# Linear attention and SwiGLU, four layers in one core: keys of two tiles from centred rows, 1/std inside phi, and phi of the last queries ahead of the first products with 1/den

## The chip, the cores and the metric

One core of a Trainium2 chip runs the whole program in one launch. The metric is device microseconds (us) of that launch; single launches of one kernel agree within about 0.3% here, and all runs below are of the fast state (granted clock 0.999 to 1.0). "PE" is TensorE, "PEld" its weight loads, "DVE" VectorE, "ACT" ScalarE, "POOL" GpSimd, "SP" SyncE, which issues most transfers. The span of a profile is some 2 us shorter than the launch time.

## The reference

Four layers on 2048 rows of 512 numbers, in bf16: linear attention (32 heads of 16), SwiGLU, and both again with the same weights.

```python
def _A_ref(x, wqkv, wo):                       # layers 0 and 2, on layernorm(x)
    q, k, v = split(x @ wqkv)                  # 32 heads of 16
    phi = lambda t: jnp.where(t > 0, t + 1, jnp.exp(t)) + 1e-6
    pq, pk = phi(q), phi(k)
    kv  = einsum("bhsd,bhse->bhde", pk, v)     # sum over all rows
    z   = einsum("bhsd->bhd", pk)              # sum over all rows
    num = einsum("bhqd,bhde->bhqe", pq, kv)
    den = einsum("bhqd,bhd->bhq", pq, z)[..., None] + 1e-6
    return (num / den) @ wo
def _B_ref(x, w_gate, w_up, w_down):           # layers 1 and 3, on layernorm(x)
    return (silu(x @ w_gate) * (x @ w_up)) @ w_down
x = x + _A_ref(_layernorm(x)); x = x + _B_ref(_layernorm(x)); ...   # twice
```

## The kernel before

The rows stand as 16 tiles of 128. The kernel is a list of operations in a fixed order: `PROGRAM` orders TensorE, and one list for each other engine orders that engine. An engine does its list strictly in order, so one instruction that waits holds up all behind it. Tokens read *layer, kind, tile*: `0k4` is the key product of tile 4 in layer 0, `t` a transpose on TensorE, `g` the sum G of (phi of keys) x rows, `q` queries, `d` den, `m` KV x Wo, `w` the output product, `u` gate and up, `n` down, `S` a dummy product that keeps the array busy. On the other engines, `0q23.phi` is the last step of phi for block 23 of the queries, `0d0.pqn2` a product of phi(q) with 1/den, `0G1.evac` a copy of G out of PSUM, `i.ld` a weight load, `i.c7` the last step of a constant mask.

```python
# layer norm of one tile (cut): statistics, then rows scaled by 1/std, then a transpose
op("dve", lambda v: v.bn_stats(...)); op("dve", lambda v: v.bn_aggr(...))        # mean, variance
op(vp_on, lambda p: p.tensor_scalar(out=vpe[:, t:t + 1], ..., scalar2=1e-5, ...)) # + eps
op("pool", lambda p: p.tensor_tensor(out=rstd[:, t:t + 1], ..., op=ALU.pow))      # ** -0.5
op("dve", lambda v: v.tensor_scalar(out=b_ap, in0=X[:, t, :], scalar1=mean,
                                    scalar2=rstd[:, t:t + 1], op0=sub, op1=ALU.mult))
# tiles 0 to 3 of layer 0 are transposed on TensorE and copied out; all others by a DMA transpose on SP

def phi(pb, dst, dk, name):
    op("act", lambda a: a.activation(out=etmp[e][:], in_=PB[pb][:], func=ACT.Exp), ...)
    if on_act:
        op("act", lambda a: a.activation(out=dst, in_=PB[pb][:], func=ACT.Identity, bias=onep[:]), ...)
    op("dve", ...)      # min(exp, 1) + 1e-6
    op("dve", ...)      # max with t + 1

# den (cut): 1/den is replicated over a head's 16 columns on ACT, transposed by DMA, multiplied on DVE
op("act", ... out=rrep ..., kind="rep"); op("sp", ... dma_start(RT..., rrep, transpose=True))
op("dve", ... out=pq, in0=pq, in1=RT, op=ALU.mult, kind="pqn")

# z (cut): Zm is z times the head mask; every den product needs it
op("dve", lambda v: v.tensor_tensor(out=Zm[:], in0=PB[pb]..., in1=mask[:]..., op=ALU.mult), kind="zm")
```

Of the kernel before, what the change touches and what calls it, by code (L numbers as in the profile page):

```python
# [164 lines left out]

PROGRAM = """
S S S S S S S S S S S S S S S S S S S S S S S S S S S S S S S S S S S S S S S S S S 0t0 S S S S S S S S 0k0 S S S S
0t1 S S S 0t2 S S S 0k1 0k2 S 0t3 0g0 0g1 0k3 0g2 0k4 0k5 0g3 0k10 0g4 0k9 0g5 0k6 0k7 0q03 0z0 0g10 0z4 0k8 0k15
0g7 0k13 0k12 0g9 0k11 0z2 0z10 0z9 0q11 0z3 0z5 0z8 0z15 0g6 0z13 0k14 0q02 0z7 0q10 0q01 0q00 0z1 0g11 0q12 0q21
0z14 0z12 0z6 0z11 0q13 0d02 0d03 0d01 0d00 0g8 0q20 0d11 0q22 0g13 0d12 0d13 0d10 0q23 0d20 0g15 0g12 0g14 0d23  # L170
0d22 0d21 0q30 0v 0q31 0m0 0m1 0m2 0m3 0r2 0w3 0w2 0q33 0w1 0w0 0w5 0w11 0q32 0w7 0w6 0w9 0d33 0w8 0w4 0w10 1u011
1u007 1u005 1u008 1u002 1u006 0d31 0d32 1u012 1u003 1u013 0d30 1u010 1u004 1u000 1u110 1u001 1u009 1n3 0w14 1n0 0w12
1u106 1n1 1u102 1n2 1u107 1u204 0w13 1u101 0w15 1u111 2k2 1u109 1u105 1u103 1u104 1u108 2k0 1u100 2k1 2q00 1u112
1u113 2k3 1n7 1u209 1n6 1u211 1u205 1n4 1n5 1u213 1u200 1u303 1u202 1u203 2q10 1u301 1u208 1u309 1u304 1u206 1u212
2g0 1u201 1u311 1u302 2q11 1u305 1u207 1u310 2q01 1u308 2q03 1u312 2q02 1u210 1n11 1u313 2k4 1u300 1n8 1n10 1u306
1n9 1u307 2k8 1n14 2k7 2k10 2k5 2q21 1n15 2k6 2k9 2k11 1n13 1n12 2q12 2k15 2k14 2g3 2g5 2q20 2q22 2k13 2q23 2g2 2k12
2g7 2g6 2g14 2q13 2s 2d01 2g12 2d02 2g1 2d00 2d03 2d20 2d13 2d21 2q30 2d22 2d10 2d12 2d11 2g13 2q31 2g10 2d23 2g15
2g4 2g9 2g11 2g8 2r1 2q32 2v 2q33 2m0 2m1 2m2 2m3 2d31 2d30 2w0 2w1 2w2 2d32 2w3 2w6 2w5 2w11 2d33 2w4 2w8 2w7 2w9
2w10 3u008 3u000 3u009 3u013 3u010 3u004 3u003 3u005 3u007 3u103 3u110 3u108 3u012 3u002 3u001 3u006 3u104 2w13
3u011 3n3 3u100 2w12 3n2 3n0 3u106 3u105 2w14 3u107 3u111 3n1 3u102 3u109 3u112 3u101 3u113 3n6 3n4 3n5 3n7 3u200  # L180
3u201 3u202 3u203 3u204 2w15 3u205 3u206 3u207 3u208 3u209 3u210 3u211 3u212 3u213 3n8 3n9 3n10 3n11 3u300 3u301
3u302 3u303 3u304 3u305 3u306 3u308 3u307 3u309 3u310 3u311 3u312 3u313 3n12 3n13 3n14 3n15
# [4 lines left out]
i.ld i.ld1 0x2.stats 0x2.sq 0x7.stats 0k0.exp 0t1.xT 0t2.xT 0x10.stats 0k1.exp 0x10.sq 0k2.exp 0t3.xT 0x15.stats  # L187
0x12.stats 0x7.sq 0k3.exp 0x15.sq 0x12.sq 0k4.exp 0k5.exp 0x13.stats 0x13.sq 0k10.exp 0k10.id1 0k9.exp 0k9.id1
0x14.stats 0x14.sq 0k6.exp 0k7.exp 0k6.id1 0q03.exp 0x11.apply 0k8.id1 0k8.exp 0k15.exp 0k15.id1 0k13.exp 0k12.exp
0k13.id1 i.c 0k11.exp 0q11.id1 i.c1 0q11.exp 0k14.id1 0k14.exp 0q02.exp 0q02.id1 0q10.exp 0q01.id1 0q01.exp 0q00.exp  # L190
i.c3 0q12.id1 0q12.exp i.c2 0q21.exp 0q21.id1 0q13.id1 0q13.exp 0d0.rep 0d0.rep2 0q20.exp 0d0.rep1 0q22.exp 0d0.rep3
0q23.exp 0q23.id1 0d1.rep1 0G0.evac 0G2.evac 0G3.evac 0d1.rep 0q30.id1 0q30.exp 0q31.exp 0q31.id1 0M1.evac 0M3.evac
0d1.rep3 0d1.rep2 1x3.sq 1x2.sq 0q33.id1 1x1.sq 0q33.exp 1x0.sq 0q32.exp 1x5.sq 0q32.id1 1x11.sq 1x7.sq 1u011.tanh
1u007.tanh 1x6.sq 1u005.tanh 1u008.tanh 1u002.tanh 1u006.tanh 1x6.apply 1x9.sq 1u012.tanh 1u003.tanh 1u013.tanh
1x4.sq 1u010.tanh 1u004.tanh 1u000.tanh 1x10.sq 0d3.rep2 1u110.tanh 1u001.tanh 0d3.rep 1u009.tanh 1x8.sq 1x10.apply
1x8.apply 1x14.sq 2x3.sq 0d3.rep1 0d3.rep3 2x1.sq 1u102.tanh 1u106.tanh 1u107.tanh 2x2.sq 1u204.tanh 1u101.tanh
2x0.sq 1x13.sq 2k2.id1 1u111.tanh 2k2.exp 1u109.tanh 1u105.tanh 1u103.tanh 2x1.apply 1u104.tanh 1u108.tanh 1x12.sq
2k0.exp 2k0.id1 2k1.id1 2q00.id1 2k1.exp 1u100.tanh 1u112.tanh 1u113.tanh 2q00.exp 1x15.sq 2k3.id1 2k3.exp 2x7.sq
1u209.tanh 2x6.sq 1u211.tanh 1x13.apply 2x4.sq 1u205.tanh 2x6.apply 1u213.tanh 2x5.sq 2x7.apply 1u200.tanh
1u303.tanh 2x5.apply 1u203.tanh 1u202.tanh 2q10.id1 2q10.exp 1u301.tanh 1u208.tanh 1u309.tanh 1u304.tanh 1u206.tanh  # L200
1u212.tanh 1u201.tanh 1u311.tanh 1u302.tanh 2q11.id1 2q11.exp 1u305.tanh 1u207.tanh 1u310.tanh 2q01.exp 2q01.id1
1u308.tanh 2q03.exp 2q03.id1 1u312.tanh 2q02.exp 2q02.id1 1u210.tanh 1u313.tanh 2k4.exp 1u300.tanh 2x11.sq 2k4.id1
2x8.sq 1u306.tanh 2x10.sq 2x8.apply 1u307.tanh 2x9.sq 2x10.apply 2x9.apply 2k8.id1 2k8.exp 2k7.exp 2x14.sq 2k7.id1
2k10.exp 2q21.id1 2k5.id1 2k5.exp 2q21.exp 2k6.exp 2x14.apply 2k9.exp 2x15.sq 2k11.exp 2k9.id1 2x13.sq 2q12.exp
2k15.exp 2x12.sq 2k15.id1 2k14.exp 2q20.exp 2k13.exp 2q22.exp 2q23.id1 2q22.id1 2k12.exp 2q23.exp 2q13.id1 2q13.exp
2d0.rep 2d0.rep1 2d0.rep2 2q31.exp 2q30.exp 2d0.rep3 2q31.id1 2d2.rep 2G0.evac 2G2.evac 2G3.evac 2q32.id1 2d2.rep1
2q32.exp 2d2.rep2 2M0.evac 2M1.evac 2M2.evac 2q33.exp 2q33.id1 2d2.rep3 3x0.sq 3x2.sq 3x1.sq 3x3.sq 3x6.sq 3x5.sq
3x11.sq 3u008.tanh 3u000.tanh 3u009.tanh 3x7.sq 3u013.tanh 3u010.tanh 3x4.sq 3u004.tanh 3u003.tanh 3u005.tanh
2d3.rep 3u103.tanh 2d3.rep1 3u007.tanh 3x9.sq 3u110.tanh 3x8.sq 3u108.tanh 2d3.rep2 3u002.tanh 3u012.tanh 3u001.tanh
2d3.rep3 3u006.tanh 3u104.tanh 3u011.tanh 3u100.tanh 3x13.sq 3x12.sq 3u106.tanh 3u105.tanh 3u107.tanh 3u111.tanh  # L210
3x10.sq 3x13.apply 3u109.tanh 3x10.apply 3u102.tanh 3u101.tanh 3u113.tanh 3u112.tanh 3u200.tanh 3u201.tanh
3u202.tanh 3u203.tanh 3u205.tanh 3u204.tanh 3u207.tanh 3u206.tanh 3u208.tanh 3u209.tanh 3x15.sq 3x14.sq 3u211.tanh
3u210.tanh 3u212.tanh 3u213.tanh 3u300.tanh 3u301.tanh 3u302.tanh 3u303.tanh 3u304.tanh 3u306.tanh 3u305.tanh
3u307.tanh 3u308.tanh 3u309.tanh 3u310.tanh 3u312.tanh 3u311.tanh 3u313.tanh
""",
    "dve": """
i.c 0x0.stats 0x0.aggr 0x0.vpe 0x1.stats 0x1.aggr 0x0.apply 0x3.stats 0t0.xT 0x4.stats 0x3.aggr 0x4.aggr 0x1.apply
0x2.apply 0x5.stats 0k0.ts 0x4.apply 0x5.aggr 0k0.phi 0x3.apply 0x9.stats 0k1.ts 0k1.phi 0x9.aggr 0k2.ts 0x5.apply
0k2.phi 0x6.stats 0x10.apply 0x6.aggr 0x9.apply 0x8.stats 0k3.ts 0k3.phi 0x7.vpe 0x6.apply 0x8.aggr 0k4.ts 0k4.phi
0x7.apply 0k5.ts 0k5.phi 0x12.vpe 0x8.apply 0k10.ts 0k10.phi 0x11.stats 0x11.aggr 0x15.apply 0x11.vpe 0x13.apply  # L220
0x12.apply 0x14.vpe 0k7.ts 0k6.ts 0k7.phi 0q03.ts 0k9.ts 0k9.phi 0k6.phi 0q03.phi 0x14.apply 0k8.ts 0k12.ts 0k15.ts
0k8.phi 0k15.phi 0k12.phi 0k13.ts 0k11.ts 0k13.phi 0k11.phi 0k14.ts 0q11.ts 0q02.ts 0k14.phi 0q11.phi 0q02.phi
0q10.ts 0q10.phi 0q01.ts 0q01.phi 0q00.ts 0q00.phi 0z.zm 0q12.ts 0d0.den 0d0.den1 0q13.ts 0q12.phi 0q13.phi 0q21.ts
0q21.phi 0q20.ts 0q20.phi 0d1.den 0q22.ts 0d1.den1 0q22.phi 0q23.ts 0d0.pqn2 0q23.phi 0G1.evac 0d0.pqn1 0d2.den
0d2.den1 0d0.pqn3 0v.mask 0q30.ts 0d2.den2 0d1.pqn1 0M0.evac 0M2.evac 0d0.pqn 0r2.pqn 0w3.res 0r2.pqn1 0w2.res
0r2.pqn2 1x3.apply 0r2.pqn3 0w1.res 1x2.apply 0w0.res 0d1.pqn3 0d1.pqn2 0q33.ts 1x1.apply 0q33.phi 0d1.pqn 0w5.res
1x0.apply 0w11.res 0w9.res 1x5.vpe 0w7.res 0w6.res 0q32.ts 1x5.apply 0w4.res 1x11.vpe 0w10.res 1x7.vpe 1u011.gst
0w8.res 1u011.h 0q31.ts 1x11.apply 0q31.phi 0q30.phi 1u007.gst 1u007.h 1x6.vpe 1u005.gst 1u008.gst 1u008.h 1u005.h
0q32.phi 1u006.gst 1u006.h 1u002.gst 1u002.h 1u012.gst 1x7.apply 1u012.h 1u003.gst 1x4.vpe 0d3.den 1x4.apply 1u003.h
1x9.apply 1u013.gst 0d3.den1 1u013.h 1u010.gst 1u010.h 1u004.gst 1u004.h 1u000.gst 1u000.h 1u001.gst 1u001.h  # L230
1u009.gst 1u009.h 1u110.gst 0d3.pqn 0d3.pqn2 0w14.res 1u110.h 1n3.res 0d3.pqn3 1n1.res 1u102.gst 1n0.res 0w12.res
# [57 lines left out]
""",  # L289
}  # L290


PE_T = set("""
0d2 0t0 0t1 0t2 0t3 2d1 2z
""".split())
# [13 lines left out]
def bass_interleave_layers__linear_attn_block__swiglu_ffn__prompt_kernel(  # L309
# [20 lines left out]
    with stack:  # L330
# [144 lines left out]
        def ln(L, t):  # L475
# [3 lines left out]
            if (L, g) not in slot_of:  # L479
                slot_of[L, g] = r_xt.take(NF if L % 2 else 2 * TG)  # L480
# [75 lines left out]
        def xt_keys(L, g):  # L556
            return [f"xt{slot_of[L, g]}_{i}" for i in range(TG)]
# [84 lines left out]
        def z_acc(L, t):  # L642
            if L not in zb:
                zb[L] = [bank(pin=True), 0]
# [280 lines left out]
```

## Time and profile before

| | before |
|---|---|
| time, median of 3 | 429.98 us (429.4 to 430.33) |
| span of the profile | 428.1 us |
| first key product starts | 7.07 us |
| key product of tile 4 starts | 15.69 us |
| last mask step ends, first den product starts | 42.20, 42.56 us |
| first output product of layer 0 (`0w`) | 56.60 us |
| sum z of layer 2 starts, G x Wqkv of layer 2 starts | 248.05, 261.35 us |
| last product starts | 424.95 us |

These start times are milestones: the same product in every variant. Times without a unit are us from the start of the profile. A difference between two kernels is read from the stretch between two milestones in which it arises. The profile lines that carry the reading stand in the prediction. One more line of the page was not thought of then and matters later. It is in the table of DMA queues (queue, kind, packets, MB, share of 16 engines), and it counts 17 instruction fetches (blocks of the program that an engine reads in) of 16 KB. I take them for TensorE's own instruction stream; the counts behind that stand below.

```profile
q8 instruction: 17, 0.28, 0.3%
```

### The profile page before, as it was taken

The numbers are of one execution on the slowest core, as the hardware profiler recorded it, in microseconds if no ns is written. First come the engines' busy times: TensorE is split into PE (matmuls) and PEld (weight loads), VectorE is DVE, ScalarE is ACT, GpSimd is POOL, SyncE is SP. The second block draws the span as 40 slices with busy tenths as digits, with TensorE's granted clock in tenths as the row PEclk, the third lists the DMA queues (instruction fetches are blocks of the program that an engine reads in).
The fourth block names the chain that finished last, engine by engine and source line by source line (L and its number), as shares of the span: only waits on it lengthen the run. The fifth ranks groups of instructions, "written<-read, shape, count | busy, mean of one in ns | idle before, by whom it ended". The sixth has DMA issues, their size and how long they took to land.

```text
span 428.1 us, 6340 instructions
## 1 busy us (share of the span) xinstructions
PE 419.4 (98%) x2219; PEld 195.5 (46%) x2219; DVE 287.8 (67%) x629; ACT 202.9 (47%) x399; POOL 83.0 (19%) x205
## 2 busy tenths in 40 slices
PE   8999899999999999999999999999999999999997
PEld 6444444444444444444444444344444444444443
DVE  6865799793675476875447869888837606853662
ACT  5998785563356264254465648445312302402220
POOL 5634035210120150001334500431002000100000
PEclk9999999999999999999999999999999999999999
DMA  8639534522011021000021113322110010021001
GB/s 277 141 75 329 126 64 101 146 50 51 4 22 37 2 52 34 2 0 2 2 48 26 25 26 63 62 46 41 38 38 0 13 51 25 0 63 37 2 0 50
DMA packets 53279, 23.21 MB, mean 54 GB/s; under 512 B 46528, under 2 KB 52160, under 8 KB 53248
## 3 DMA queue, kind: packets, MB, share of 16 engines
q1 hardware_dynamic: 51408, 16.27, 17.6%
q0 software_dynamic: 1296, 6.03, 4.1%
q10 hardware_dynamic: 544, 0.52, 0.4%
q8 instruction: 17, 0.28, 0.3%
q14 instruction: 14, 0.11, 0.1%
HBM read 9.70 MB, written 2.10 MB: 28 GB/s over the span
## 4 chain that ended last, share of the span: by engine, by line
PE 88%; DMA 5%; ACT 3%; DVE 2%; issue 1%; SPq 0%; POOL 0%; ACTq 0%; DVEq 0%
PE pb L409 88%; DMA RT<-rrep 2%; DMA xnT<-xnA 1%; DMA X<-in_A_x_dram 1%; ACT pq L567 1%; ACT etmp L564 1%; ACT rrep L719 0%; DVE pq L573 0%; ACT GT L657 0%; DVE pq L732 0%; SPq L723 0%; ACT xnA L498 0%; SPq L440 0%; DVE xnA L522 0%; ACT xnA L495 0%
## 5 line engine op out<-in xcount | busy, mean ns | idle before, releaser
L782 ACT ACTIVATE tht<-pb 128x512 f32<-128x512 f32 x112 | 65.4, 595 | 129.4 <-PE pb L409 106.8
L409 PE MATMUL pb<-xnT,Wg 128*128 128x512 bf16 x448 | 115.0, 379 | 0.6 <-issue 0.6
L409 PE MATMUL pb<-xnT,Wu 128*128 128x512 bf16 x448 | 115.0, 379 | 0.0
L784 DVE SCALAR_TENSOR_TENSOR tht<-tht,pb 128x512 f32<-128x512 f32 x112 | 75.4, 684 | 55.6 <-ACT tht L782 48.9
L409 PE MATMUL pb<-Wd,hT 128*128 128x512 bf16 (+2 forms) x462 | 99.8, 373 | 0.0
L787 DVE TENSOR_TENSOR hT<-tht,pb 128x512 bf16<-128x512 f32 x112 | 74.2, 682 | 2.8
L409 PEld LDWEIGHTS pb<-Wd,hT 128*128 128x128 bf16 x462 | 44.7, 98 | 52.3 <-DVE hT L787 0.2
L409 PEld LDWEIGHTS pb<-xnT,Wu 128*128 128x128 bf16 x448 | 43.6, 98 | 53.1 <-DVE hT L787 0.8
L409 PEld LDWEIGHTS pb<-xnT,Wg 128*128 128x128 bf16 x448 | 43.5, 98 | 53.3 <-issue 1.3
L511 POOL TENSOR_TENSOR rstd<-vpe,negh 128x1 f32<-128x1 f32 x64 | 37.4, 587 | 90.4 <-DVE vpe L507 88.3
L564 ACT ACTIVATE etmp<-pb 128x512 bf16<-128x512 f32 x64 | 37.2, 594 | 21.8 <-PE pb L409 13.1
L501 POOL TENSOR_SCALAR mv<-sums 128x1 f32<-128x1 f32 x55 | 12.8, 239 | 119.8 <-DVE X L810 62.1
L409 PE MATMUL pb<-Wqkv,xnT 128*128 128x512 bf16 x128 | 31.2, 379 | 1.2 <-DMA xnT<-xnA 0.6
L409 PE MATMUL pb<-xnT,Wqkv 128*128 128x512 bf16 x128 | 32.1, 379 | 0.0
L409 PE MATMUL pb<-pk,xnA 128*128 128x512 bf16 x128 | 31.2, 379 | 0.0
L409 PE MATMUL pb<-GT,pq 128*128 128x512 bf16 x128 | 30.2, 379 | 0.2
L498 ACT ACTIVATE xnB<-X,sums 128x512 bf16<-128x512 bf16 x32 | 22.9, 717 | 15.7 <-DVE X L762 8.8
L569 DVE TENSOR_SCALAR etmp<-etmp 128x512 bf16<-128x512 bf16 x64 | 18.7, 304 | 12.1 <-ACT etmp L564 12.0
L762 DVE SCALAR_TENSOR_TENSOR X<-pb,X 128x512 bf16<-128x512 f32 x32 | 21.6, 686 | 7.1 <-PE pb L409 7.0
L810 DVE SCALAR_TENSOR_TENSOR X<-pb,X 128x512 bf16<-128x512 f32 x16 | 11.0, 689 | 19.1 <-PE pb L409 19.0
L498 ACT ACTIVATE xnA<-X,sums 128x512 bf16<-128x512 bf16 x23 | 16.5, 717 | 12.1 <-DVE X L810 11.9
L810 DVE SCALAR_TENSOR_TENSOR pq<-pb,X 128x512 bf16<-128x512 f32 (+2 forms) x17 | 10.9, 656 | 14.4 <-PE pb L409 14.3
(77 smaller groups left out, 309.9 us busy)
## 6 DMA issues: line engine op xcount, KB each, us to landing
out_dram<-pq SPq DMA_DIRECT2D x15, 128.0 KB, 1.8
Wg<-in_B_w_gate_dram POOLq DMA_DIRECT2D x4, 448.0 KB, 4.9
Wu<-in_B_w_up_dram POOLq DMA_DIRECT2D x4, 448.0 KB, 4.6
X<-in_A_x_dram SPq DMA_DIRECT2D x6, 256.0 KB, 4.8
Wd<-in_B_w_down_dram POOLq DMA_DIRECT2D x3, 512.0 KB, 4.7
Wqkv<-in_A_wqkv_dram SPq DMA_DIRECT2D x2, 512.0 KB, 7.0
Wqkv<-in_A_wqkv_dram ACTq DMA_DIRECT2D x2, 256.0 KB, 3.5
X<-in_A_x_dram SPq DMA_DIRECT2D x4, 128.0 KB, 3.4
```

The lines of the kernel that those rows point to most:

```text
L409: return op("pe", lambda e: e.matmul(o_ap, lhsT=lhsT, rhs=rhs, start=start, stop=stop, skip_group_check=skip), r=r, w=w, n=n)
L498: op("act", lambda a: a.activation(out=b_ap, in_=X[:, t, :], func=ACT.Square, scale=-float(D), bias=sums[:, t:t + 1], accum_out=mv[:, t, 1 ...
L501: op("pool", lambda p: p.tensor_scalar(out=mv[:, t, 0:1], in0=sums[:, t:t + 1], scalar1=-1.0 / D, scalar2=None, op0=ALU.mult), r=[f"sm{t}" ...
L511: op("pool", lambda p: p.tensor_tensor(out=rstd[:, t:t + 1], in0=vpe[:, t:t + 1], in1=negh[:], op=ALU.pow), r=[f"vp{t}", "negh"], w=[f"rs{ ...
L564: op("act", lambda a: a.activation(out=etmp[e][:], in_=PB[pb][:], func=ACT.Exp), r=[f"pb{pb}"], w=[f"e{e}"], kind="exp")
L567: op("act", lambda a: a.activation(out=dst, in_=PB[pb][:], func=ACT.Identity, bias=onep[:]), r=[f"pb{pb}", "onep"], w=dk, kind="id1")
L569: op("dve", lambda v: v.tensor_scalar(out=etmp[e][:], in0=etmp[e][:], scalar1=1.0, scalar2=1e-6, op0=ALU.min, op1=ALU.add), r=[f"e{e}"], w ...
L762: op("dve", lambda v: v.scalar_tensor_tensor(out=X[:, t, :], in0=PB[pb][:], scalar=1.0, in1=X[:, t, :], op0=ALU.mult, op1=ALU.add, accum_o ...
L782: op("act", lambda e: e.activation(out=tht[a][:], in_=PB[pg][:], func=ACT.Tanh, scale=0.5), r=[f"pb{pg}"], w=[f"th{a}"], kind="tanh")
L784: op("dve", lambda v: v.scalar_tensor_tensor(out=tht[a][:], in0=tht[a][:], scalar=1.0, in1=PB[pg][:], op0=ALU.add, op1=ALU.mult), r=[f"pb{ ...
L787: op("dve", lambda v: v.tensor_tensor(out=hT[h][:, j, :], in0=tht[a][:], in1=PB[pu][:], op=ALU.mult), r=[f"pb{pu}", f"th{a}"], w=[f"h{h}_{ ...
L810: op("dve", lambda v, pb=pb, lo=lo, hi=hi: v.scalar_tensor_tensor(out=o_ap[:, lo:hi], in0=PB[pb][:, 0:hi - lo], scalar=0.5, in1=X[:, t, lo ...
```

## The change

Its intent: start the first key products earlier by leaving 1/std out of the way to them; take away the stop of 1.33 us near 50 us; shorten the waits around z and the output product of layer 2.

```diff
+            if f"{L}c{t}" in PE_T:                      # tiles 0 and 1 of layer 0: rows minus mean only
+                op("dve", lambda v: v.tensor_scalar(out=pq[3][:, t, :], in0=X[:, t, :], scalar1=mean, scalar2=None, op0=sub), ...)
...
-        def phi(pb, dst, dk, name):
+        def phi(pb, dst, dk, name, by=1.0, rk=()):      # by = rstd of the tile
-            op("act", lambda a: a.activation(out=etmp[e][:], in_=PB[pb][:], func=ACT.Exp),
+            op("act", lambda a: a.activation(out=etmp[e][:], in_=PB[pb][:], func=ACT.Exp, scale=by),
-                op("act", lambda a: a.activation(out=dst, in_=PB[pb][:], func=ACT.Identity, bias=onep[:]),
+                op("act", lambda a: a.activation(out=dst, in_=PB[pb][:], func=ACT.Identity, bias=onep[:], scale=by),
...
 PROGRAM, head ("S*42" stands for 42 tokens S)
-S*42 0t0 S*8 0k0 S*4 0t1 S*3 0t2 S*3 0k1 0k2 S 0t3 0g0 0g1 0k3 0g2 0k4
+S*27 0c0 S*8 0k0 S*3 0c1 S*3 0t2 0k1 0t3 S*3 0k2 0k3 S 0g0 0g1 0g2 0k4
 PROGRAM, layer 2
-2s 2d01 2g12 2d02 ... 2m3 2d31 2d30 2w0 2w1 2w2
+2s 2g12 2d01 2d02 ... 2m3 2w0 2d31 2d30 2w2 2w1
 order of VectorE, layer 0
-0d1.den 0q22.ts 0d1.den1 0q22.phi 0q23.ts 0d0.pqn2 0q23.phi 0G1.evac 0d0.pqn1 0d2.den 0d2.den1 0d0.pqn3 0v.mask
+0d1.den 0d1.den1 0q23.ts 0q22.ts 0q22.phi 0d0.pqn 0q23.phi 0G3.evac 0d2.den 0d0.pqn2 0d2.den1 0d0.pqn1 0v.mask
 order of ScalarE, layer 0
-0q22.exp 0d0.rep3 0q23.exp 0q23.id1 0d1.rep1 0G0.evac 0G2.evac 0G3.evac 0d1.rep
+0q22.exp 0q23.exp 0q23.id1 0d0.rep3 0G0.evac 0G2.evac 0G1.evac 0d1.rep1 0q30.id1 0d1.rep
... (cut: the head of the other lists, layer 2's keys and queries, layer 3; two more DMA transposes, 0x0.xT and 0x1.xT)
```

## The prediction

> **What bounds the kernel now.** I read the page's busy table first, then its chain of waits, then the waits of PE alone, then the PE, DVE and ACT timelines where the chain leaves PE.
>
> ```profile
> PE 419.4 (98%) x2219; PEld 195.5 (46%) x2219; DVE 287.8 (67%) x629; ACT 202.9 (47%) x399; POOL 83.0 (19%) x205
> ...
> PE 88%; DMA 5%; ACT 3%; DVE 2%; issue 1%; SPq 0%; POOL 0%; ACTq 0%; DVEq 0%
> ```
>
> PE is the bound: 98% busy and 88% of the chain that ended last. The 98% contains dummy products at the start (42 in one piece, `pb<-hT`) that only keep the array running, so PE's free time is better counted from the timeline. In steady state four 128x512 products start every 0.864 us (123.73, 124.59, 125.45), 0.216 us each. Adding the column counts of all matmuls other than the dummies at 2.4 GHz gives 407 us. So of the 428.1 us span about 21 us is not needed by the products. Some 7 us of it lie before the first key product at 7.07, 3 us after the last matmul start (424.9), and the rest is dummies, per-matmul overhead (2.5 ns x 2000 = 5 us) and waits. The waits are what a change of order can win:
>
> ```profile
> PE pb L409 <- DVE pq L573: 1.3, 1, 1.3
> ...
> PE pb L409 <- DMA xnT<-xnA: 0.6, 1, 0.6
> PE pb L409 <- DVE xnT L553: 0.5, 1, 0.5
> PE pb L409 <- DVE GT L633: 0.4, 1, 0.4
> PE pb L409 <- DVE Zm L614: 0.4, 1, 0.4
> PE pb L409 <- DVE pq L750: 0.3, 1, 0.3
> ```
>
> The first, 1.3 us, is the largest wait of PE in the kernel and falls at 50.5. The chain of waits (start, length, piece) and below it the timeline (start, length, engine, line, operands, idle before) show where it comes from:
>
> ```profile
> 46.51 4.53 DMA RT<-rrep
> 51.04 0.02 issue
> 51.06 0.04 DVE pq L732
> 51.10 0.31 issue
> 51.40 0.43 DVE pq L573
> ```
>
> ```profile
> 51.06 0.43 DVE L732 TENSOR_TENSOR pq<-pq,RT 128x512 bf16<-128x512 bf16 x1 [1.83 <-DMA RT<-rrep]
> ...
> 51.40 0.42 DVE L573 TENSOR_TENSOR pq<-pq,etmp 128x512 bf16<-128x512 bf16 x1
> ...
> 51.88 0.46 PE L409 MATMUL pb<-Zm,pq 128*128 128x8 bf16 x12 [1.33 <-DVE pq L573]
> ```
>
> DVE works in program order. The last step of phi of query 23 (L573, 0.42 us) had its inputs by 49.4, but stands behind a product with 1/den (L732) that waits for the second transposed 1/den tile, landed at 51.04. DVE stood idle for 1.83 us and PE with it. ACT too: its copies of G (L657) began at 51.64, behind a replicate (L719) that waited for a buffer held by the same transpose. That transpose took longer than its neighbours (48.79 to 51.04 from its first to last engine, others 0.15 to 0.2 us); one 16 KB instruction fetch ran on a DMA engine just then. So part of this wait is luck.
>
> At the head, the chain runs over loads and the first DMA transpose:
>
> ```profile
> 9.80 5.84 DMA xnT<-xnA
> 15.65 0.05 issue
> 15.69 25.94 PE pb L409 x176
> ```
>
> From 15.69 PE runs dense to 42. What counts at the head is therefore when the key product of tile 4 starts, and how much was finished before it.
>
> **What the Trainium skill says.**
> - "TensorE: Matmul & The Clock Gate", Part 1: back to back products start every 107 ns for 128 columns while the clock is cold and every 55.6 (128) or 215.7 ns (512) warm, and the array warms after some 3.4 us of sustained work. The trace agrees: the dummies start 107 ns apart until 5.27 us, then 56 ns; 512 columns take 216 ns.
> - "ScalarE: Activation LUTs", What ACT_TABLE_LOAD costs: each per-partition pointer operand adds about 93 ns to an ACTIVATE. The trace agrees: exp with immediates is 0.60 us, Identity with a pointer bias 0.68. Exp with 1/std as scale should be near 0.68, Identity with both near 0.78.
> - "DMA: Bandwidth & Descriptors", Queues, rings and completion order: descriptors on an engine's ring are taken in ring order. The trace agrees as far as it shows: the first transpose is issued at 9.80, but the last weight load on the same queue lands at 13.74 and the transpose at 15.65.
>
> **The change, part by part.**
> 1. *Keys of tiles 0 and 1 from centred rows.* For the first tile it takes out, on the path to the keys, the +eps (0.15 us), the power on POOL (0.55) and the scaling (0.38), and puts one subtraction on DVE (estimate 0.38, from the same-size L522). Before: statistics end 4.22, scaled rows 5.66, PE transposes 5.72, copy 6.52 to 6.93 (it queued behind statistics on DVE), product 7.07. After: subtraction 4.25 to 4.63, transposes 4.7 to 5.1, copy on ACT (0.58) to 5.75, product at about 5.8. So the first key product starts 1.25 us earlier. The 27 dummies now end at 4.13 (27 x 107 ns after 1.24); about 0.5 us of idle array follows.
>    Cost: two exps and two Identities with a pointer scale (4 x 0.09 us on ACT), two subtractions on DVE (0.8 us), and two additional DMA transposes, since queries still need scaled rows of tiles 0 and 1 (14 instead of 12, 1.2 us of issue each).
>    Does it reach tile 4? In both orders four keys and three G groups stand ahead of it (7 x 0.864 = 6.0 us). Adding DVE's and ACT's durations in the new order I get: key 1 at 9.0 (its transposed copy waits on ACT behind statistics of tile 4), keys 2 at 10.6, copy of tile 3 on ACT to 12.0 (behind tile 10's statistics), key 3 at 12.0, G 0 to 2 until 15.5 to 15.7. Tile 4's transpose, now second in the queue behind tile 1's, lands at 15 to 16.4. So tile 4 starts near 15.7, where it did. The 1.25 us are given back. I put the head at 0, give or take 0.6.
> 2. *phi ahead of the first product with 1/den, layer 0.* DVE now has only product 0 (first transpose, landed 47.63 before) ahead of phi of query 23, and 3 copies of G stand ahead of the replicate for the next group on ACT. The 1.33 us wait goes; then the copies of G set the pace: G's products end at 50.4, three ACT copies at 0.52 us end at about 52.0, against 53.2. The matmuls with G move from 53.05 to about 51.8. Gain 1.2 to 1.5 us, I take 1.3. It holds to the next block if the transposes of layer 1 move along: the last one landed at 68.46, 0.34 us before its product at 68.80, and its chain (X, statistics, apply) starts from the same moved products. The later replicates now follow the copies, at about 52.5, which only uses slack.
> 3. *Layer 2, sum z.* PE waits 0.41 (L633) and 0.39 (L614) at 248. One G group (0.86 us) moves between the sum and the first use of Zm and covers the second. DVE takes one 0.69 us addition from POOL (1.15 us there), while phi of key 12 gets its Identity from ACT, about 0.2 us later. Gain 0.3.
> 4. *Layer 2, first Wo product before two den products, and the residual of tile 3 before the product with 1/den.* PE waits of 0.28 (L750, 264.5) and 0.59 at 276 (the transposes of layer 3; the fourth landed 276.39). Residual 3 no longer sits behind a transpose that landed at 269.93; I work out its transpose 0.4 us earlier. Together 0.6.
> 5. *The rest* (Identities moved between ACT and DVE, four more applies on ACT in layer 3): beside a dense PE with DVE 67% and ACT 47% busy; 0.
>
> Sum: 0 + 1.3 + 0.3 + 0.6 = 2.2 us of 430: 427.8.
>
> **Rivals.**
> - *The two more transposes starve the head.* For it: SP issues one per 1.3 us, and PE used tile 10 only 0.7 us and tile 7 0.3 us after landing. If all later tiles come 2.6 us later, PE loses 1 to 2 us and the total is about 429.5. Against it: SP was idle from 11.1 to 12.9, and the queue is blocked by loads until 13.7, so issues before that cost only data time (about 0.7 us each).
> - *The head keeps its gain* (ACT less late than I add up): 1.2 us more, 426.6.
> - *The wait at 50 stays in another place*: the mask of KV stands behind the third transpose, and the fetch may hit another one. Then 0.5 us of gain remain there, 428.6.
> - *A cold clock.* The idle 0.5 us could delay the warm clock by a window: key 0 takes 1.7 us instead of 0.86, which ends before key 1 in any case. No effect.
>
> **Range and chances.** The useful products need 407 us plus overhead, so no order can win 2% (8.6 us) here; nothing added could lose that much either. The rivals span 426.6 to 429.5; with the spread of runs (429.4 to 430.33) I take 427.7, with 425.9 to 429.4.
>
> **What would show it.** Right: first key product at 5.8 but tile 4's still near 15.7; no PE wait on L573's successor near 50; the G products near 51.8; the first gate product near 67.3 instead of 68.8; only one of the two waits at 248. Wrong: tile 4 starting before 15 or after 16.5, PE gaps among the keys between 16 and 42, or a new PE wait on 1/den's transposes near 55 or 270 that eats part 2 or 4.

## More of the kernel before

GpSimd's list at the end of layer 0's head is `0x14.pow 0x14.negm i.ld i.ld1 i.ld2 ... i.ld8 i.c7 1x3.negm`: nine weight loads, and behind them the last step of the mask. The first four loads are issued one after the other (31.36 to 33.42 us); each later one waits until an earlier one has landed.

## The result, and the profile after

The changed kernel is correct. In four launches it took 429.5 us (429.39 to 430.48), the kernel before beside it 429.69 (429.4 to 430.33). Ratio 0.9999, interval 0.9979 to 1.0018. (A ratio is the mean time of one kernel's fast runs over that of the other's of the same rounds, so it is not quite the ratio of the medians.) The time did not move, and the expected 2.2 us did not arrive.

The page of the changed kernel has the same bound. PE is busy 98% of the span; its share of the chain that ended last fell from 88 to 85%:

```profile
PE 418.2 (98%) x2203; PEld 193.8 (45%) x2203; DVE 288.9 (68%) x626; ACT 205.7 (48%) x399; POOL 84.7 (20%) x212
...
PE 85%; DMA 6%; DVE 3%; ACT 3%; issue 1%; SPq 0%; POOL 0%; POOLq 0%; DVEq 0%; ACTq 0%
```

PE's waits (who waits, for what: us in total, times, longest) are not fewer, they are others. The 1.3 us for `pq L573` are gone. New are 0.9 us for a product with 1/den (L759), 0.8 and 0.5 us in the head (L549), 0.7 us for Zm, and 0.2 us for the mask of KV:

```profile
PE pb L409 <- DVE pq L759: 0.9, 1, 0.9
PE pb L549 <- DVE vpe L511: 0.8, 1, 0.8
PE pb L409 <- DVE Zm L642: 0.7, 1, 0.7
PE pb L549 <- DVE xnA L526: 0.5, 1, 0.5
...
PE pb L409 <- DVE KVT L696: 0.2, 1, 0.2
```

**Where the gain came.** DVE's timeline (start, length, engine, line, operation, operands) near 50 us shows the product with 1/den (L759) and, right behind it, the finish of phi (L593), with no idle time between them:

```profile
50.35 0.42 DVE L759 TENSOR_TENSOR pq<-pq,RT 128x512 bf16<-128x512 bf16 x1
50.69 0.42 DVE L593 TENSOR_TENSOR pq<-pq,etmp 128x512 bf16<-128x512 bf16 x1
```

PE's timeline there has no stop at 50. Its new stop, 0.22 us, stands ahead of KV x Wo, as the third rival had named:

```profile
51.28 0.45 PE L409 MATMUL pb<-Zm,pq 128*128 128x8 bf16 x12
...
52.45 1.06 PE L409 MATMUL pb<-GT,Wqkv 128*128 128x128 bf16 x16
...
54.59 0.81 PE L409 MATMUL pb<-Wo,KVT 128*128 128x512 bf16 x3 [0.22 <-DVE KVT L696]
```

**Where it went.** Cut at the milestones, all in us. The second column of the changed kernel is a second profile of it, taken later:

| stretch | before | changed | changed, again |
|---|---|---|---|
| start to the first den product | 42.56 | 43.43 | 43.98 |
| to the first output product of layer 0 | 14.04 | 12.53 | 12.54 |
| to the sum z of layer 2 | 191.45 | 192.53 | 192.07 |
| to G x Wqkv of layer 2 | 13.30 | 12.47 | 12.47 |
| to the last product | 163.60 | 163.97 | 164.00 |

So the middle gained 1.5 us and the stretch behind z 0.8. But the head lost 0.9 to 1.4, the keys of layer 2 some 0.9 (inside the third stretch, shown below), and the end 0.4.

The head can be followed line by line. The first key product starts at 5.79 as predicted, but the transposes of tiles 2 and 3 wait for DVE, and tile 4's product starts at 15.92, 0.2 us later than before:

```profile
8.53 0.40 PE L549 MATMUL pb<-ident,xnA 128*128 128x128 bf16 x4 [0.76 <-DVE vpe L511]
...
10.57 0.40 PE L549 MATMUL pb<-ident,xnA 128*128 128x128 bf16 x4 [0.54 <-DVE xnA L526]
...
15.92 1.89 PE L409 MATMUL pb<-Wqkv,xnT 128*128 128x512 bf16 x8
```

That is about what the prediction said, down to the price of the pointer operands (exp with 1/std takes 0.68 us, Identity with two pointers 0.78). What it had not seen comes at 42 us. In GpSimd's timeline of the kernel before, the last weight loads are issued one by one, each after a wait of 0.5 to 0.8 us for an older one to land, and the mask follows:

```profile
38.84 0.54 POOL L440 DMA_DIRECT2D Wu<-in_B_w_up_dram  x1 [0.49 <-DMA Wu<-in_B_w_up_dram]
...
41.83 0.37 POOL L430 TENSOR_SCALAR_AFFINE_SELECT mask<-mask 128x128 bf16<-128x128 bf16 x1
```

In the changed kernel the same load waits 1.95 us, and the mask comes 0.94 us later:

```profile
39.97 0.54 POOL L440 DMA_DIRECT2D Wu<-in_B_w_up_dram  x1 [1.95 <-DMA Wu<-in_B_w_up_dram]
...
42.77 0.36 POOL L430 TENSOR_SCALAR_AFFINE_SELECT mask<-mask 128x128 bf16<-128x128 bf16 x1
```

Before, Zm was computed 0.10 us after the mask was ready, so there was no slack. Here are the first den products, before (no wait) and in the changed kernel, where PE stands until Zm is there:

```profile
42.56 0.56 PE L409 MATMUL pb<-Zm,pq 128*128 128x8 bf16 x16
...
43.43 0.59 PE L409 MATMUL pb<-Zm,pq 128*128 128x8 bf16 x16 [0.70 <-DVE Zm L642]
```

Why does the load wait? The trace has the landing of every transfer for each of the 16 DMA engines. The load in question had landed on 15 engines by 38.32 and on the last at 39.69 (before: 38.40 and 38.55). One instruction fetch of 16 KB began at 36.56 and took 1.11 us. Before, the same fetch ran at 32.8, when nothing urgent was moving. TensorE reads about 260 recorded instructions per fetch (2,219 products and 2,219 weight loads over 17; between the second and the seventeenth fetch it starts 249); no other engine has nearly as many (VectorE 629). The page "Runtime: NRT & Kernel Launch", Instruction fetch mechanics, in the Trainium skill says that streams are refilled in 16 KiB blocks of 256 instructions by the sequencer's own queue; the trace agrees in the size and nearly in the count, and does not show whose queue it is. Sixteen dummies fewer are 32 TensorE instructions fewer, so later fetches should come later in time. Most do, but not all: the third lies at 49.27 (before 49.03), the fourth at 68.77 (69.83), the eleventh at 251.71 (251.82). So the theory has a testable cause: the *number of dummies*, not anything that computes.

The traces allow a count over all fourteen profiles of this document. Of 1,188 DMA transposes, 26 landed on their last engine 1.5 to 2.1 us after the fifteenth, and for all 26 a fetch of 16 KB was running between 0.8 us before the first landing and the last. Another 22 were 0.5 to 0.93 us behind: each of them met a fetch of 8 KB on queue q14, and none met one of 16 KB. Of the other 1,140, at most 0.5 us behind, only 5 met a 16 KB fetch in that span.

### The profile page after: what moved, and what is told of

It is laid out like the page before. It is cut to its first block, busy times and chain, and to the rows that moved or that the text cites. A ratio compares the mean times of both kernels' runs of the same rounds, so it can differ in the third digit from the quotient of the medians.

```text
span 427.8 us, 6315 instructions
## 1 busy us (share of the span) xinstructions
PE 418.2 (98%) x2203; PEld 193.8 (45%) x2203; DVE 288.9 (68%) x626; ACT 205.7 (48%) x399; POOL 84.7 (20%) x212
## 4 chain that ended last, share of the span: by engine, by line
PE 85%; DMA 6%; DVE 3%; ACT 3%; issue 1%; SPq 0%; POOL 0%; POOLq 0%; DVEq 0%; ACTq 0%
PE pb L409 85%; DMA xnT<-xnB 1%; DMA Wu<-in_B_w_up_dram 1%; DMA Wo<-in_A_wo_dram 1%; DMA X<-in_A_x_dram 1%; DMA RT<-rrep 1%; ACT etmp L584 1%; DMA xnT<-xnA 1%; ACT pk L587 0%; SPq L440 0%; ACT xnA L498 0%; DVE pk L596 0%; DVE KVT L696 0%; ACT xnA L495 0%; DVE etmp L589 0%
## 5 line engine op out<-in xcount | busy, mean ns | idle before, releaser
L584 ACT ACTIVATE etmp<-pb 128x512 bf16<-128x512 f32 x62 | 36.1, 598 | 22.3 <-PE pb L409 13.9
L409 PE MATMUL pb<-Wqkv,xnT 128*128 128x512 bf16 x120 | 29.5, 379 | 0.6 <-issue 0.3
L589 DVE TENSOR_SCALAR etmp<-etmp 128x512 bf16<-128x512 bf16 x64 | 19.8, 319 | 14.0 <-ACT etmp L584 13.8
L498 ACT ACTIVATE xnA<-X,sums 128x512 bf16<-128x512 bf16 x21 | 15.1, 717 | 16.1 <-DVE X L837 16.0
```

The lines of the kernel that those rows point to most:

```text
L409: return op("pe", lambda e: e.matmul(o_ap, lhsT=lhsT, rhs=rhs, start=start, stop=stop, skip_group_check=skip), r=r, w=w, n=n)
L498: op("act", lambda a: a.activation(out=b_ap, in_=X[:, t, :], func=ACT.Square, scale=-float(D), bias=sums[:, t:t + 1], accum_out=mv[:, t, 1 ...
L589: op("dve", lambda v: v.tensor_scalar(out=etmp[e][:], in0=etmp[e][:], scalar1=1.0, scalar2=1e-6, op0=ALU.min, op1=ALU.add), r=[f"e{e}"], w ...
```

## The experiments

Each part of the change can be taken alone, because the orders are lists: a variant takes the stretch of one kernel's lists and the rest of the other's. All were correct and all had five rounds beside the kernel before.

### The changed kernel again, and each part alone

```diff
 after_again: the changed kernel, unchanged
 head_only:   before, with the changed lists up to 0q20 (centred keys, 45 dummies)
 mid_only:    before, with the changed lists from 0q20 to layer 1 (phi ahead of the products with 1/den, copies of G ahead of replicates)
 l2_only:     before, with the changed lists from layer 2 on
```

> The changed kernel once more, to tell order from luck. Theory G (given back): the waits that took the place of the removed one follow from the order, so they come again: PE waits about 0.7 us for Zm at 42.4 because the last step of the mask stands on POOL behind the issue of the weight loads; key product of tile 12 about 0.4 us late at 243.6; about 0.9 us for a product with 1/den at 269.8. Theory L (luck): they come from transfers that a fetch of instructions happened to slow, so at least two of the three change by more than 0.3 us in this profile. Time 429.5, ratio 0.999 to 1.001 under both.

> Keys of tiles 0 and 1 from centred rows, and the rest of the changed head up to the last product of query 20, with the order of before from there. Theory G: first key product at 5.8 instead of 7.07, but tile 4's key product at 15.9 (before 15.69), so ratio 1.000 (0.999 to 1.001), and the 1.3 us wait at 50 is there. Rival H (the head gains and something later eats it): tile 4's product before 15.0 in some executions and ratio below 0.998.

> The order of the changed kernel only between query 20 of layer 0 and the middle of layer 1 (phi of query 23 ahead of the second product with 1/den, copies of G ahead of the replicate); head and layers 2 and 3 as before. Theory G: Zm's product at 42.6 as before, the 1.3 us wait gone, the first product of G with Wqkv at 51.6 to 51.9 instead of 53.05, the first gate product at 67.5 instead of 68.80, and since layers 1 to 3 follow that, ratio 0.997 (about 1.2 us). Rival S (slack later: what layer 0 wins, later stages bound by transfers give away): the first gate product 1.2 us earlier, but layer 3's first gate product still within 0.3 us of 276.5, ratio 0.999 to 1.001.

> The order and placement of the changed kernel in layers 2 and 3 alone, on the head and layer 0 of before. Theory G: about 0.9 us of the two waits at 248 goes, but key 12 waits 0.4 us more, the product with 1/den near 270 waits 0.7 us more, and the first gate product of layer 3 starts within 0.3 us of before's 276.5: ratio 1.000. Prediction's parts 3 and 4: 0.9 us, ratio 0.998.

| run | median us (range) | ratio to before, interval |
|---|---|---|
| after_again | 430.24 (429.66 to 431.19) | 1.0018, 1.0004 to 1.0032 |
| head_only | 432.29 (431.34 to 433.52) | 1.0063, 1.0046 to 1.0079 |
| mid_only | 428.44 (428.08 to 428.59) | 0.9972, 0.9959 to 0.9986 |
| l2_only | 429.64 (429.14 to 429.86) | 1.0000, 0.9988 to 1.0013 |

The middle part is worth 1.2 us, as the prediction's second step said (1.3). Layer 2 is worth nothing. The head costs 2.7 us when it stands alone, which no theory of mine had expected (the interval of head_only lies wholly above the 0.999 to 1.001 that I wrote down). In head_only the first den product starts at 44.28 instead of 42.56: tile 4's product starts at 16.59 (before 15.69), and PE waits 0.60 us for Zm. The end is 0.7 us longer (164.30 instead of 163.60). Part of the loss may come from a cold array, one that still runs at half pace: this line is four key products in 1.87 us, almost twice the usual 1.02:

```profile
6.37 1.87 PE L407 MATMUL pb<-Wqkv,pq 128*128 128x512 bf16 x4
```

The changed kernel's own profile has 1.02 us there, so the clock is not what it lost by. The second profile of the changed kernel (after_again) has the same three new waits as the first: 0.77 us for Zm (first 0.70), 0.29 for key 12 (0.29), 0.65 for the product with 1/den (0.89). None moved by more than 0.3, so theory G's forecast held: they come again with the program. (Theory L's mechanism, transfers slowed by fetches, turns out to be right as well; only the chance in it is not.) In all three profiles with the new head the second fetch lies at 36.6 to 37.3; in before, mid_only and l2_only at 32.6 to 32.8.

l2_only shows what layer 2 did. The stretch behind z takes 12.47 instead of 13.30 us (0.83 gained), but from layer 0's output product to z it takes 192.13. Counted from the start of one product to the start of the next, less 0.216 (some 0.17 us more than the brackets of the profile show), key products there wait 0.24, 0.17 and 0.51 us near 235, 240 and 243 that before does not have; in the changed kernel the same three take 0.29, 0.12 and 0.46. So 0.83 came and 0.87 to 0.92 went, ahead of the place where it came.

### One move of the middle part

```diff
 order of VectorE, layer 0 (all else is before)
-0q23.ts 0d0.pqn2 0q23.phi 0G1.evac
+0q23.ts 0q23.phi 0d0.pqn2 0G1.evac
```

> The kernel before with one thing moved: on VectorE the finish of phi of the last query block of channel group 2 (0q23) stands ahead of the first product with 1/den (0d0.pqn2) instead of behind it. Theory: the stop of 1.50 us at 50.2 goes, the 1/den products of column block 2 begin near 50.6 instead of 51.8, but nothing behind them comes earlier: the copies of G to SBUF on ScalarE stand behind the copies of the replicated 1/den in its order, so the first product of G with Wqkv still begins near 53.05, and the time stays (ratio 0.998 to 1.001). Rival: the move alone carries the gain that the middle part showed (-1.2 us), ratio 0.996 to 0.998, first product of G with Wqkv near 51.5.

Measured: 429.49 us (429.05 to 430.05), ratio 1.0000, 0.9987 to 1.0013. PE's stop at 50 is gone and the time stays, as expected. My reason was half right. G x Wqkv starts at 51.71, not at 53.05; but it then waits piece by piece for ACT's copies of G, which still stand behind replicates:

```profile
51.71 0.28 PE L407 MATMUL pb<-GT,Wqkv 128*128 128x128 bf16 x2
52.20 0.23 PE L407 MATMUL pb<-GT,Wqkv 128*128 128x128 bf16 x1 [0.20 <-ACT GT L682]
52.69 0.90 PE L407 MATMUL pb<-GT,Wqkv 128*128 128x128 bf16 x13 [0.26 <-ACT GT L682]
```

The first output product starts at 56.04, 0.56 us earlier than before, where mid_only has 54.92. So the wait that the page named first was the smaller half; the other half is ACT's order. The 0.8 us by which its profile ends earlier do not show in five rounds: launches of one kernel spread by as much.

### The mask ahead of the loads

```diff
 order of GpSimd (mid_mask on mid_only, after_mask on the changed kernel)
-i.ld i.ld1 i.ld2 i.ld3 i.ld4 i.ld5 i.ld6 i.ld7 i.ld8 i.c7
+i.c7 i.ld i.ld1 i.ld2 i.ld3 i.ld4 i.ld5 i.ld6 i.ld7 i.ld8
```

> The kernel before with the middle part of the change (mid_only), and on GpSimd the last step of the causal mask ahead of the nine weight loads that GpSimd issues, instead of behind them. Theory: the wait of 0.22 us for Zm at 42.1 goes, the first product of den begins near 42.1 to 42.4, everything after is 0.1 to 0.25 earlier than in mid_only, as long as the loads behind the mask are no later than their use; ratio 0.9965 against before. Rival: the loads come 1 to 2 us later and the first weights of layer 1 wait, ratio 0.998 or more.

> The changed kernel, with the last step of the causal mask ahead of the nine weight loads on GpSimd. Theory: of the three places at which the changed kernel gives its gain back, the wait for Zm at 42.4 (0.87 us) goes; d00 begins near 42.5 instead of 43.4, G with Wqkv near 51.6, and the last product ends 0.6 to 0.9 us earlier than in the changed kernel: ratio against before 0.998. Rival: the wait is not owned by the mask but by phi of the late keys or by another step of Zm: d00 stays at 43.2 or later and the ratio stays 1.000.

mid_mask took 428.84 us (428.42 to 429.81), ratio 0.9985, 0.9973 to 0.9997; after_mask 429.81 (428.47 to 430.8), ratio 1.0002, 0.9987 to 1.0017. Both are misses. The wait for Zm did go: neither profile has one, and the mask is ready at 25.9 and 28.9. But in after_mask a key product waited 0.89 us until 23.98, because a fetch at 21.7 met the transpose that it needed (landed on 15 engines from 22.08 to 22.27, on the last at 23.93), and the den products began at 43.72. In mid_mask the wait for tile 4's transpose was 1.04 us instead of none above 0.1. The mask is the place where the delay shows, not its source, and moving it gave nothing that the rounds can tell.

### The number of dummies, both ways

```diff
 after_spin: PROGRAM of the changed kernel, 61 dummies again
-... 0c1 S*3 0t2 0k1 0t3 S*3 0k2 0k3
+... 0c1 S*12 0t2 0k1 S*7 0t3 S*3 0k2 0k3
 fewspin: PROGRAM of the kernel before, 45 dummies
-S*42 0t0 S*8 0k0 S*4 0t1 S*3 0t2 S*3 0k1 0k2 S 0t3
+S*42 0t0 0k0 0t1 0t2 S*2 0k1 0k2 S 0t3
```

> The changed kernel with 16 more dummy products at the head (61 as before has, 9 of them ahead of the transpose of tile 2 and 7 ahead of tile 3), so that TensorE's instruction count at each later place is that of before. Theory: the 16 KB fetch that lay at 36.6 us among the weight loads goes back to about 33, the loads land as before, the last mask step is back near 41.9, the first den product near 42.6, and the ratio is 0.997 to 0.999. Rival: the mask is late for another reason that the head brings (the order of the transfers or of GpSimd); then the last mask step stays at 42.7 or later though the fetch moves, and the ratio is 1.000 or, if the dummies delay the keys, more.

> The kernel before with only 16 of its 61 dummy products taken out, those between the first transpose and the fourth (45 left, as many as in the changed kernel). Nothing that computes is touched. Theory: the 16 KB fetches move with TensorE's instruction count, from 13.5 and 32.8 us to 18 to 21 and 36 to 38; the second lies among the weight loads, the last mask step ends 0.5 to 1.5 us later (42.4 to 43.3), the first den product begins at 43.0 or later (42.56 before), while the wait for tile 4's transpose at 14.7 shrinks because no fetch meets it; ratio 1.000 to 1.003. Rival: the late mask of the changed kernel came of its new order of transfers and copies; then the mask stays at 41.7 to 42.0 here. A third outcome: the clock cools for want of dummies, seen as first key products 427 ns apart.

after_spin took 428.95 us (428.67 to 429.77), ratio 0.9987, 0.9975 to 0.9999, against 1.0018 and 0.9999 for the changed kernel. Its fetches are at 14.1 and 33.3, the last mask step starts at 42.13, and there is no wait for Zm. Adding work that computes nothing made it 0.5 to 1.3 us faster, as the theory said; the interval lies below that of after_again, and overlaps the wide one of the first four launches. It did not bring all back: the first den product starts at 43.04 (changed 43.43 and 43.98, before 42.56), because tile 4's product starts only at 16.27, when its transpose has landed (16.03 to 16.23).

fewspin took 432.52 us (432.13 to 433.01), ratio 1.0069, 1.0056 to 1.0082: 3 us slower for sixteen dummies less, and more than I had expected. The fetches moved to 15.0 and 38.7: later, though I had expected 18 to 21 and 36 to 38. The first key product starts at 7.08, as before (7.07), and tile 4's at 14.88, 0.8 us earlier than before. But the transpose of tile 5 met the fetch at 14.99. It landed on 15 engines by 15.35 and on the last at 17.24, and PE stands for it:

```profile
17.29 1.04 PE L409 MATMUL pb<-Wqkv,xnT 128*128 128x512 bf16 x4 [1.37 <-DMA xnT<-xnA]
```

GpSimd's timeline shows the held load and the late mask, in a kernel in which no transfer, copy or order was touched:

```profile
41.85 0.54 POOL L440 DMA_DIRECT2D Wg<-in_B_w_gate_dram  x1 [2.03 <-DMA Wg<-in_B_w_gate_dram]
...
43.52 0.37 POOL L430 TENSOR_SCALAR_AFFINE_SELECT mask<-mask 128x128 bf16<-128x128 bf16 x1
```

PE's timeline has the wait for Zm, 1.02 us. The keys are not cold: four products from 13.09 take 1.03 us. So the first den product starts at 44.26, 1.70 us later than before:

```profile
44.26 0.56 PE L409 MATMUL pb<-Zm,pq 128*128 128x8 bf16 x16 [1.02 <-DVE Zm L614]
```

The other part of its loss is at the end: from G x Wqkv of layer 2 to the last product it takes 164.88 instead of 163.60. A fetch at 269.5 met a transpose of 1/den issued at 268.31, which landed at 272.29 to 272.61, and PE waits 1.38 us behind it. What no run did is to keep the number of dummies and move only their places.

Over the twelve kernels with 61 or 45 dummies the sorting is complete:

| dummies | kernels | second fetch at | last mask step ends (behind the loads) | near-266 fetch at |
|---|---|---|---|---|
| 61 | before, mid_only, l2_only, phi_only, after_spin, mid_tail | 32.6 to 33.3 | 42.0 to 42.5 | 264.8 to 265.9 |
| 45 | changed (twice), head_only, fewspin | 36.6 to 38.7 | 43.1 to 44.0 | 267.5 to 269.5 |

(The three with the mask moved have their fetch in the same groups: mid_mask 33.2; after_mask 37.8 and order_fix 38.0.) The last column is the same effect at the other end (in head_only and fewspin, work itself is 1.4 to 1.5 us late at the sum z). In the changed kernel the fetch at 267.53 came upon a transpose of 1/den issued at 266.41, which landed at 270.17 to 270.47, late on all engines; in after_spin, with the fetch at 265.3, the same transpose took from 265.88 to 268.31. The wait of PE behind it is 0.89 us in the changed kernel, and none above 0.1 in after_spin. But there PE then waits 0.57 us at 275.78 for a transpose of layer 3, and the stretch to the last product takes 163.88 us against 163.97. So the dummies gave back only 0.1 of the 0.4 us that the changed kernel loses at the end.

### The two late tiles in the head

```diff
 order of VectorE (on after_mask)
-0x3.vpe 0x6.stats 0x4.apply 0k0.ts 0x3.apply
+0x3.vpe 0x6.stats 0x3.apply 0x4.apply 0k0.ts
 order of ScalarE
-0x10.stats 0x10.sq 0t3.xT
+0t3.xT 0x10.stats 0x10.sq
```

> The changed kernel with the last mask step ahead of the weight loads (after_mask) and two moves in the head: on VectorE the normalisation of tile 3 ahead of that of tile 4 and of the finish of the first phi, on ScalarE the copy of tile 3's transpose ahead of the statistics of tile 10. Theory: the head's early first key (5.8) did not reach tile 4 because tile 3 came late through these two orders (TensorE idle 0.76 and 0.54 us before the transposes of tiles 2 and 3); with them mended tile 4's product begins at 15.2 to 15.5 instead of 15.9 to 16.0, and the den products at 42.3 to 42.9 where no fetch meets a transpose at 20 to 23. Ratio 0.998 (0.9965 to 0.9995). Rival: tile 4's product is bound by the transfer that holds its transpose; it stays at 15.8 or later, ratio 1.000.

A miss: 430.55 us (429.87 to 431.33), ratio 1.0024, 1.0009 to 1.0038. Tile 4's product came at 16.56, later than in any other kernel but head_only (16.59). What was taken from tile 3 was paid by phi of the first keys: the G products now wait for their last steps, and a transpose met by the fetch at 17.7 costs a further 0.69 us:

```profile
14.00 0.39 PE L406 MATMUL pb<-pk,xnA 128*128 128x512 bf16 x1 [0.26 <-ACT pk L584]
14.68 2.04 PE L406 MATMUL pb<-pk,xnA 128*128 128x512 bf16 x8 [0.29 <-DVE pk L590]
```

So mending these two orders does not help. In the changed kernel ACT is busy for 5.97 and DVE for 5.28 of the 6 us from 8 to 14; I take it that they have too much to do there for the earlier first key to reach tile 4, but no run tests that.

### The tail of layer 2 without its keys

```diff
 mid_tail: mid_only, and from the sum z on the changed lists; keys and queries of layer 2 as before
-2s 2d01 2g12 2d02 ... 2m3 2d31 2d30 2w0 2w1 2w2
+2s 2g12 2d01 2d02 ... 2m3 2w0 2d31 2d30 2w2 2w1
 (and VectorE and ScalarE behind it: residuals and phi ahead of products with 1/den)
```

> The kernel before with the middle part of the change (mid_only) and, of the layer-2 part, only what follows the sums over keys: G of tile 12 ahead of the first den product, the order of 1/den and phi, Wo with tiles 0 and 2 first, and the residuals behind it. The keys and their order stay those of before. Prediction's step: the wait of TensorE ahead of the first gate product of layer 3 (0.6 to 1.0 us in mid_only and its like) goes, 0.6 us less than mid_only, ratio 0.9957. Theory now: the two waits ahead of that product trade with each other (the product with 1/den near 269 and the gate near 275); their sum stays at 0.7 to 1.2 us; ratio 0.9965 to 0.998, as mid_only.

427.60 us (427.31 to 428.1), ratio 0.9957, 0.9944 to 0.9970: 0.65 us below mid_only, and better than both kernels. The prediction's number was met, but not for its reason; my theory's range (0.9965 to 0.998) was missed by the ratio, though not by its interval. The stretch behind z takes 12.78 instead of 13.30: the G product of tile 12 now runs while Zm is computed, so the second of the two waits at z is covered. The first one remains:

```profile
247.57 0.25 PE L406 MATMUL pb<-ones,GT 128*128 128x1 bf16 x4 [0.41 <-DVE GT L670]
247.68 1.02 PE L406 MATMUL pb<-pk,xnA 128*128 128x512 bf16 x4
248.54 0.34 PE L406 MATMUL pb<-Zm,pq 128*128 128x8 bf16 x8
```

That is 0.52 us. The stretch from there to the last product takes 163.35 instead of 163.54, only 0.19 us. There the waits changed places, as the theory had said: ahead of the output products stand 0.79 us instead of 0.28, and the 0.78 us ahead of the gate of layer 3 are gone.

### More dummies

```diff
 more_spin: mid_tail, 73 dummies, and the mask ahead of the loads
-S*42 0t0 S*8 0k0
+S*46 0t0 S*16 0k0
```

> mid_tail (the kernel before with the middle part and the layer-2 tail) with 12 more dummy products in two waits that TensorE has anyway (4 ahead of the first transpose, 8 ahead of the first key), 73 in all, and the last mask step ahead of the weight loads. Theory: the fetches move the other way, by 12 products: the first from 13.2 to 10.5 to 12.3 us, the second from 32.6 to 29.5 to 31.5. The first then no longer meets the transpose of tile 4 as it lands, so tile 4's product begins at 14.8 to 15.3 instead of 15.5 to 15.8; the mask does not hold the den products (they begin near 41.9 to 42.2); ratio 0.9945 against before (0.9935 to 0.996; mid_tail 0.9957), unless the second fetch meets one of the last transposes near 30 us, which would show as a wait there. Rival: the times of the fetches are not tied to TensorE's instruction count, the first stays at 13 to 14 us, tile 4 at 15.5 to 15.8, ratio as mid_tail or up to 0.001 above, since the dummies and the later loads cost a little.

428.51 us (427.79 to 429.48), ratio 0.9976, 0.9963 to 0.9990: a miss in the time and in the fetch. The fetches moved in the direction expected, but by 0.4 us only, to 12.8 and 32.2; tile 4's product stayed at 15.57. Its profiled launch was its fastest and ended 0.15 us ahead of mid_tail's, with den products at 42.28; over six launches it is slower than mid_tail. So the time of a fetch is tied to the count of instructions, but not by a rule that I can compute with. Two parts were changed at once here, and I cannot say which one costs.

## Why the prediction was wrong

The sum was 0 + 1.3 + 0.3 + 0.6 = 2.2 us. In the profiles the middle came (1.5), and three things took it back: the head (0.9 to 1.4 lost where 0 was expected), the keys of layer 2 (0.9 lost), and the end (0.4 lost where 0.6 was to be won). By the prediction's own steps:

1. **Head, "0, give or take 0.6": this step failed.** Its mechanism was right as far as it went: first key at 5.79, copies of tile 3 late on ACT, tile 4's product at 15.92. It stopped there. It took tile 4's start as the only thing that counts at the head, and saw in the dummies only their length ("the 27 dummies now end at 4.13"). The runs showed 0.87 and 1.42 us lost at the first den product; of the first, 0.23 stood at tile 4 and 0.64 between tile 4 and den, where the prediction had counted on a dense run and PE now waits 0.70 for Zm. The dummies alone move this: fewspin lost 1.70 us there, and after_spin was 0.39 and 0.94 us earlier than the changed kernel, with 0.48 still lost. At the end fewspin lost 1.28 us, but after_spin won back only 0.1 of 0.4; the rest of that loss stays open. That the road leads over the instruction fetch is shown by the profiles as far as profiles can: the held load is late on one DMA engine of sixteen, just after a fetch, and the count over fourteen profiles finds transposes so late only beside fetches. No run could forbid a fetch. Even the kernel before paid one such toll at the head: the transpose of tile 4 landed on fifteen engines from 13.97 to 14.14 and on the last at 15.65, with a fetch at 13.48. The changed kernel had no fetch there and its transpose was in at 14.82, but its keys were not ready for it.
2. **phi ahead of the product with 1/den, 1.3 us: right.** mid_only measured 1.2 us in launches and 1.3 in the profile's last product. phi_only shows that it takes both halves, the move on VectorE and the copies of G ahead of the replicates on ACT, which the step had said. The mask of KV gives 0.1 to 0.2 us back, as the third rival said. In mid_only PE also stands 0.48 us near 80 (0.30 in the changed kernel). The transpose ahead of that place, through which the changed kernel's chain of waits runs too, lands at 78.53 there and at 78.41 before, though it was issued 1 us earlier: so it seems that the gain cannot pass it whole.
3. **Sum z, 0.3 us: mechanism right, sizes wrong on both sides.** The second wait was covered (0.5), and the first shrank (0.3), so 0.83 came. Against it the term "phi of key 12 ... about 0.2 us later" measured 0.87 us: three key products of layer 2 wait. Net 0. Without the new order of the keys, mid_tail keeps 0.5.
4. **Output product of layer 2, 0.6 us: this step failed too; the stretch lost 0.37.** The wait at 276 did go (0.59 to none in the changed kernel). But 0.49 us for the copy of G and 0.89 us for the product with 1/den took its place: a wait "near 270", which the prediction had named as what would make it wrong. mid_tail (163.35) and l2_only (163.42 us for the stretch, before 163.60) keep 0.2 of the gain.
5. **The rest, 0:** not tested alone; the stretches leave nothing over that needs it.

The rivals: the two extra transposes did not starve the head (tile 4's transpose landed at 14.82, more than 1 us before PE came for it); the head did not keep its gain; the cold clock appeared in head_only (1.87 us for the first four key products) and in part in after_spin (1.43). The prediction saw one 16 KB fetch lengthen a transpose in the kernel before and called it luck. It was right about the size of such a collision and wrong about luck: where the fetches lie depends on the program, and in twelve of the fourteen profiles the same transpose of 1/den (on fifteen engines by 48.9 to 50.6) meets the third fetch. Its 407 us for the products hold (965,704 columns at the measured 0.216 us per 512) and already contain the overhead that its range adds to them; nothing rests on that.

What stays open: why removing 16 products moves the second fetch by 4 to 6 us, the third by 1.4 on average, and adding 12 moves the second by only 0.4; whether the places of the dummies count beside their number; and how much of head_only's loss is its cold array.

## What to carry to other kernels

Taking instructions out can cost time: a change of the instruction count can move later fetches of that engine (in fewspin by 1 to 9 us), and a fetch that meets a transpose or a load on the way to the bound holds it up by a microsecond or two (1.5 to 2.1 in the 26 cases here). Look for the transfer whose last engine lands far behind the other fifteen. Test each part of a reordering alone and keep the parts that pay: here two of the four gave 427.6 us, while all four together gave nothing. And a constant that is made behind a chain of loads, used 0.1 us after it is ready, is a wait in waiting, though moving it alone won nothing here.

## What the Trainium skill lacked or had wrong

- "Runtime: NRT & Kernel Launch", Instruction fetch mechanics, calls the cost of crossing a 16 KiB boundary mostly hidden. TensorE itself was never seen to wait for one, but what lands beside such a fetch (0.9 to 1.6 us) is late on one DMA engine of sixteen: a weight load from 38.32 to 39.69, a transpose from 22.27 to 23.93. Sixteen dummy products fewer, with such delays in the profile, cost 0.69%.
- No page says that dummy products move the fetches. With 61 dummies the second lay at 32.6 to 33.3 us, with 45 at 36.6 to 38.7.
- "DMA: Bandwidth & Descriptors", Queues, rings and completion order, puts the refill of instructions on row 14. Here 17 pieces of 16 KB ran on the queue that the profile calls q8, and 14 pieces of 8 KB on q14; no run here shows whether these numbers are the page's rows.
